# Attention with a gated feed-forward part on one Trainium2 core: two of three pattern operands of a score group added by an accumulating DMA

## The chip, the cores and the metric

The kernel runs on one core of a Trainium2 chip. A core has five engines that run their own instruction lists and wait for one another through semaphores: TensorE (PE; matmuls, its weight loads shown as PEld), VectorE (DVE), ScalarE (ACT), GpSimd (POOL) and SyncE (SP), which here only issues DMAs. Sixteen DMA engines move the data. The metric is the device time of one execution in microseconds, lower is better; the time given is the median of three runs.

## The reference

One block on 2048 tokens of width 512, all arrays bf16: a layer norm, then attention with 32 heads of width 16 and a gated feed-forward part of width 1792 beside it, both added to the input.

```python
def _A_ref(x, wqkv, wo):
    B, S, D = x.shape            # 1, 2048, 512
    H = 32; Dh = D // H          # 16
    qkv = (x @ wqkv).reshape(B, S, 3, H, Dh).transpose(2, 0, 3, 1, 4)
    q, k, v = qkv[0], qkv[1], qkv[2]
    scores = jnp.einsum("bhqd,bhkd->bhqk", q, k) * (Dh ** -0.5)
    p = _softmax(scores, axis=-1)
    o = jnp.einsum("bhqk,bhkd->bhqd", p, v)
    return o.transpose(0, 2, 1, 3).reshape(B, S, D) @ wo

def _B_ref(x, W_gate, W_up, W_down):
    gate = jnp.einsum("bsd,df->bsf", x, W_gate)
    up = jnp.einsum("bsd,df->bsf", x, W_up)
    h = gate * (gate > 0) * up
    return jnp.einsum("bsf,fd->bsd", h, W_down)

xn = _layernorm(x)
return x + _A_ref(xn, A_wqkv, A_wo) + _B_ref(xn, B_W_gate, B_W_up, B_W_down)
```

## The kernel before

**The work.** Attention is cut into 32 blocks: four stretches of 512 queries (`c4`), four sets of eight heads (`gg`), and two halves of each set (`ee`), so that a block has four heads. A block goes through 16 tiles of 128 keys (`kt`). For one key tile TensorE makes the scores of four heads, each 128 keys by 512 queries, in one PSUM bank of float32. The array is used in tiles of 64 rows by 32 columns: a score of one head is four matmuls in one half of the array, and the other half runs another one beside it. `matmul_loaded` (L136) issues one such matmul whose weights are already loaded; its tile size is fixed at 64x32.

**Two ways through the softmax.** A key tile takes one of two ways.

- *ScalarE.* Two exponentials (L1525) of 128x1024 each, `units` in the code, read two score banks each and write a slot of `ring`, a ring of `NRING` slots of 128x1024 bf16. Four matmuls in each half of the array then multiply the two slots with the values (`pv_stream`, L1405) and add into the block's PSUM bank. There are 708 such units.
- *VectorE.* The key tiles that `QUADS` and `dve_kt` choose, 158 in all (five in most blocks, six in six of them), go through `quad` (L1473), called a group here. Four instructions (L1481) turn four score banks into int16 numbers whose bits, read as bf16, are a power of two with a linear mantissa. Adding a constant to these bits gives the same curve shifted, and the sum of three shifted curves comes close to the exponential. So a group has three patterns of 128x2048: `raw`, `xa` (`raw` + 31) and `xb` (`raw` + 81). The two additions are made on GpSimd as 64-bit integer additions (L1495, `p3`), but on VectorE (L1498) for the first `FIRSTD` and last `LASTD` groups, two each. Each pattern is then multiplied with the values by itself, so the sum of the three curves is made in PSUM: three calls of `pv_stream`, 3 x 8 matmuls a group.

`raw` has `NRAW` = 4 slots and the other patterns `NPAT` = 5, all in the tensor `qd` (L650), 4 KB per partition and slot. A ring slot is 2 KB per partition.

**The other work.** Into the gaps go the projections of queries, keys and values, the feed-forward part (weights streamed in by SyncE's DMAs), the output projection, and at each block's end its normalisation, whose row sums come out of the value matmul.

**The order.** Nothing is ordered by hand. Every operation is entered with an engine, an estimated duration, what it reads and writes, and a priority. `Graph.run` (L212) then plays the program through: at each step the engine that can start earliest takes an operation, and with it buffer slots from the pools. A consumer of a GpSimd result may start at the producer's planned end (start, duration, latency `lat`) plus a slack; `PAT_SLACK`, 100 ns, for the value matmuls of a group. [...] `Graph.emit` (L443) writes the queues out as they were planned, with the semaphore waits that are needed. Each engine then runs its list strictly in that order, whatever the real durations are. SyncE's DMAs have a `stream` each, whose semaphore counts 16 for each transfer; `emit` recognises a DMA by its engine, `o.eng == "SP"`.

A group is entered `AHEAD` = 10 units before the unit at which its key tile stands, and its value matmuls have a priority one behind that unit.

**The opening.** TensorE starts with `heat` (L1018), ten matmuls of 128x128 weights and 512 columns of zeros into a bank that nobody reads; the plan gives it 4.5 us. While nothing else can run, `run` puts further blank matmuls of that kind into gaps (L1543). Then come the transposes of the normalised input (L858), the first projections and the first scores.

Of the kernel before, what the change touches and what calls it, by code (L numbers as in the profile page):

```python
# [5 lines left out]
BF16 = mybir.dt.bfloat16  # L6
# [6 lines left out]
ALU = mybir.AluOpType  # L13
# [13 lines left out]
EPS = 1e-5  # L27

BANK = (6, 7, 2, 3)
NRING = 16  # L30
PV_LAG = 1
BG_PRIO = 2
D1_PRIO = -500.0
# [10 lines left out]
NQ = 2  # L44
NWS = 2
NRAW = 4
NPAT = 5
LEAD = 15
QOFF = 0.3
EARLY = ()  # L50
# [3 lines left out]
FIRSTD = 2  # L54
TOGETHER = 0
LAST2 = 1
LASTD = 2
# [24 lines left out]
PV_EARLY = False  # L82
POOL_NS = 1060
LIB_NS = 7000
LANES = 0x0001000100010001
QUADS = [0, 3, 4, 5, 5, 6, 5, 5, 5, 5, 6, 5, 5, 5, 5, 6, 5, 5, 5, 6, 5, 5, 5, 5, 6, 5, 5, 5, 5, 6, 5, 5]

# [45 lines left out]
                 "load", "wsrc", "wkey", "wwaits", "pair")  # L133


def matmul_loaded(e, out, w, x, start, stop, at):  # L136

    return e.add_instruction(mybir.InstMatmult(  # L138
        name=e.bass.get_next_instruction_name(), engine=mybir.EngineType.PE, ins=[e.lower_ap(x), e.lower_ap(w)], outs=[e.lower_ap(out)],
        start_tensor_calc=start, stop_tensor_calc=stop, tile_size=(64, 32), tile_position=at, ldweights=False))  # L140


class Graph:
# [299 lines left out]
    def emit(self, nc, es):  # L443
        order = sorted(self.ops, key=lambda o: (o.start, o.idx))
        for o in self.ops:
            o.signal = o.eng == "SP"
            o.hb = None

        sems = {c: es.enter_context(nc.semaphore("s_" + c.lower())) for c in ("PE", "PEhi", "ACT", "DVE", "POOL")}
# [10 lines left out]
                held[o.half] = o.wkey  # L460

        def line(o):
            return o.stream if o.eng == "SP" else "PEhi" if o.eng == "PE" and o.half else o.eng
        for e in self.ENGS:
            n = {}
            for o in self.queue[e]:
# [10 lines left out]
        while left:  # L477
            moved = False
            for e in self.ENGS:
                q = self.queue[e]  # L480
                while pos[e] < len(q):
                    o = q[pos[e]]
                    if any(d.hb is None for d in o.deps):
                        break
                    k = known[e]
                    need = []
                    if e == "PE" and o.wsrc and o.load is not None:
                        o.wwaits = []
                        for d in sorted(o.wsrc, key=lambda d: -d.seq):
                            c = line(d)  # L490
                            v = d.val if d.eng == "SP" else d.cseq
                            if loads.get(c, -1) >= v:
                                continue
                            o.wwaits.append(d)
                            d.signal = True
                            for cc, vv in d.hb.items():
                                loads[cc] = max(loads.get(cc, -1), vv)
                                k[cc] = max(k.get(cc, -1), vv)
                    for d in sorted(o.deps, key=lambda d: -d.seq):
                        c = line(d)  # L500
                        v = d.val if d.eng == "SP" else d.cseq
                        if k.get(c, -1) >= v:
                            continue
                        need.append(d)
                        for cc, vv in d.hb.items():
                            if k.get(cc, -1) < vv:
                                k[cc] = vv
                    o.waits = need
                    for d in need:
                        d.signal = True  # L510
                    if e == "SP":
                        o.val = streams.get(o.stream, 0)
                        streams[o.stream] = o.val + 1
                        h = dict(k)
                        h[o.stream] = o.val
                    else:
                        h = dict(k)
                        h[line(o)] = o.cseq
                    o.hb = h
                    pos[e] += 1  # L520
                    left -= 1
                    moved = True
            assert moved, "cyclic order"
        dsem = {s: es.enter_context(nc.semaphore("d_%d" % i)) for i, s in enumerate(streams)}
        for e in self.ENGS:
            v = {}
            for o in self.queue[e]:
                if e == "SP":
                    o.sem = (dsem[o.stream], 16 * (o.val + 1))
                elif o.pair is not None:  # L530

                    o.sem = (pairs[o.pair % 2], 2 * (o.pair // 2 + 1))
                elif o.signal:
                    v[line(o)] = v.get(line(o), 0) + 1
                    o.sem = (sems[line(o)], v[line(o)])
# [11 lines left out]
        def play(e, eng):  # L547
            def wait(ds):
                best = {}
                for d in ds:  # L550
                    s, v = d.sem
                    if id(s) not in best or best[id(s)][1] < v:
                        best[id(s)] = (s, v)
                for s, v in best.values():
                    eng.wait_ge(s, v)
            loaded = set()
            for i, o in enumerate(self.queue[e]):
                if e == "SP" and i == end:
                    for s, v in done:
                        eng.wait_ge(s, v)  # L560
                if e == "PE" and o.load and o not in loaded:
                    wait(o.wwaits)
                    o.load(eng)
                if e == "PE" and o.load is not None and o.waits:

                    for q in self.queue[e][i + 1:i + 1 + self.AHEAD_LOADS]:
                        if q.load is None or q.wwaits or q in loaded:
                            break
                        if q.half != o.half:
                            if q.load:  # L570
                                q.load(eng)
                                loaded.add(q)
                            break
                wait(o.waits)
                ins = o.fn(eng)
                if e == "SP" or o.name == "st":
                    ins.then_inc(o.sem[0], 16)
                elif o.signal or o.pair is not None:
                    ins.then_inc(o.sem[0], 1)
            if e == "SP":  # L580
                for s, v in fin:
                    eng.wait_ge(s, v)
# [23 lines left out]
def bass_parallel_sum__mha_block__glu_gated_reglu__prompt_kernel(  # L606
# [13 lines left out]
    with ExitStack() as es:  # L620
        def sb(name, shape, dt):
# [20 lines left out]
        Wo_l = sb("Wo_l", [128, 2, D], BF16)  # L642
# [18 lines left out]
        ps = es.enter_context(nc.psum_tensor("ps", [128, 8, 512], FP32))  # L661

        G = Graph()
# [19 lines left out]
        zeros = Wo_l[:, 0, :]  # L683
# [5 lines left out]
             reads=[t_pid], writes=[t_pid], prio=-890)  # L689
        for v in (0, 2, 1, 3):  # L690
            G.op("DVE", 100, lambda e, v=v: e.tensor_scalar(hmask[:, v:v + 1], pid[:, 0:1], 16.0 * v, QSCALE, op0=ALU.is_equal, op1=ALU.mult),
                 reads=[t_pid], writes=[t_masks[v]], prio=-889 + v)
# [4 lines left out]
             reads=[t_id], writes=[t_id], prio=-898)  # L697
# [71 lines left out]
        for j in range(4):  # L769
            for ee in range(2):  # L770
                r0 = 32 * j + DH * ee
                dma(lambda e, r0=r0, ee=ee: e.dma_start(Wo_l[r0:r0 + DH, ee, :], A_wo[D - 128 + r0:D - 128 + r0 + DH, :]), 16,
                    reads=[t_woz], writes=[Tile()], prio=60, after=100)
# [4 lines left out]
        acc, junk = warm, up_sb[:, 0, 0:D // 2].bitcast(BF16)  # L778
# [213 lines left out]
        for n, bk in enumerate(blocks):  # L992
            q = QUADS[n]
            dve_kt[bk] = [int((a + QOFF) * NT / q * (LAST_QUADS if n == len(blocks) - 1 else 1.0)) for a in range(q)] if n else EARLY
            if n:
                at = sorted({min(max(t + QUAD_SHIFT.get((n, a), 0), 0), NT - 1) for a, t in enumerate(dve_kt[bk])})
                if len(at) == len(dve_kt[bk]):
                    dve_kt[bk] = at
        kinds = {}
# [5 lines left out]
        at_unit, n = [], 0  # L1005
# [11 lines left out]

        def heat(e):  # L1018
            ins = None
            for _ in range(10):  # L1020
                ins = e.matmul(ps[:, BANK[0], :], Wo_l[:, 0, 0:128], zeros, start=True, stop=True)
            return ins
        G.op("PE", 4500, heat, reads=[t_zero], writes=[t_pvz], prio=-900)
        ln_block(0, -800)
        pb = Tile("pro", P_b, [3])
# [31 lines left out]
        for v in (0, 2, 1, 3):  # L1057
# [3 lines left out]
            for n, (tile, bank, c, x) in enumerate(((pb, 3, slice(0, 384), slice(0, 384)), (bq, 1, slice(128, 256), slice(384, 512)))):  # L1061
# [4 lines left out]
                     reads=[tile, t_masks[v]], writes=[] if n else [t1], joins=[q0], prio=MASK_LATE + v if late else -787 + 0.2 * v + 0.1 * n,  # L1066
# [153 lines left out]
        at, rest = 40.0, sum(j[1] for j in seq[:-4])  # L1220
        for w, n, fn, lead in seq:
            at = max(at, w)
# [250 lines left out]
        def quad(key, u, prev):  # L1473
# [4 lines left out]
            for j in SC_ORDER:  # L1478
# [4 lines left out]
                    reads=[tx], joins=[tq], prio=D1_PRIO, name="d1")  # L1483
# [5 lines left out]
            ta, xa = made("qa")  # L1489
            tb, xb = made("qb")  # L1490
            nq[0] += 1
            for n, (t, x) in enumerate(((ta, xa), (tb, xb))):
                share, off = ((POOL1_SHARE, P1_OFF), (POOL_SHARE, 0.0))[n] if FIRSTD < nq[0] <= len(kinds) - LASTD else (0.0, 0.0)
                if int(nq[0] * share + off) > int((nq[0] - 1) * share + off):
                    G.op("POOL", POOL_NS, lambda e, x=x, n=n: e.int64_add(x().bitcast(I64), raw().bitcast(I64), SHIFTS[n + 1] * LANES),  # L1495
                        reads=[ti, tq, t_lib], writes=[t], prio=u, name="p3", port=True)
                    continue
                G.op("DVE", 600, lambda e, n=n, x=x: e.tensor_scalar(x(), raw(), float(SHIFTS[n + 1]), None, op0=ALU.add),  # L1498
                     reads=[ti, tq], writes=[t], prio=u, name="d%d" % (n + 2), port=True)
            first = len(G.ops)  # L1500
            for t, x, more in ((ti, raw, [tq]), (ta, xa, []), (tb, xb, [])):
                pv_stream(key[:3], key[3], [(lambda rows, j=j, x=x: x()[rows, 512 * j:512 * j + 512].bitcast(BF16)) for j in range(4)],
                          [t] + more, u, u + PV_LAG, "DVE")
            if TOGETHER:
# [2 lines left out]
                        o.order |= set((ta if TOGETHER == 1 else tb).w)  # L1507
            return prev

        nq = [0]  # L1510
        quads = sorted((at_unit[place[k]], place[k], k) for k in kinds)
        prev_sc, prev_d, made_q = None, None, 0
        for u, unit in enumerate(units):
            while li < len(plan) and plan[li][0] <= u:
# [4 lines left out]
            key, p = unit[:4], unit[4]  # L1519
            k0 = u % 2  # L1520
            ts = Tile("s%d" % u, P_sc, [k0])
            for sub in range(2):
# [3 lines left out]
                              reads=[ts], writes=[tr], prio=u - 100, order=[exp_ops[u - 1]] if u else [], name="ex%d" % u)  # L1526
# [54 lines left out]
```

## Time and profile before

| what | value |
|---|---|
| median of three runs | 684.08 us (683.42 to 684.76) |
| the profiled execution, whole | 682.77 us |
| its span, first to last instruction | 680.6 us |
| granted TensorE clock, mean | 1.00 |
| DMA: moved; mean rate | 28.77 MB; 42 GB/s |
| first exponential starts; last ends | 10.3 us; 669.5 us |

The profile is one execution. Its span leaves out what lies before the first and after the last instruction. A busy time counts the time in which at least one instruction of the engine runs, so instructions that overlap in the pipeline are not counted twice: the mean duration of one exponential, 1117 ns, is longer than its share of the busy time, 651.9 / 708 = 0.921 us. In a group's row the idle time stands behind the bar, with the instruction that ended most of it. PE, PEld, DVE, ACT, POOL and SP are the engines as named above.

### The profile page before, as it was taken

The page shows a single profiled execution, that of the slowest core. Times are in us where ns is not written, and L with a number is a line of the kernel's source. Part 1 is how long each engine was busy: PE and PEld are TensorE (multiplying, and loading weights), DVE is VectorE, ACT ScalarE, POOL GpSimd, SP SyncE. Part 2 cuts the span into 40 slices and gives each one's busy share as a digit, 9 for nine tenths or more (in the row PEclk, how much of TensorE's full clock was granted, in tenths as well). Part 3 has the DMA queues.
Part 4 walks back from the last instruction along what each step waited for, and adds up shares of the span by engine and source line. Part 5 has one row for each costly group of instructions (what it writes and reads, how often), then busy time and mean ns, then how long its engine had stood idle before and what let it go on. Part 6 is the DMA issues. An engine that isn't in the chain of part 4 may idle for free.

```text
span 680.6 us, 46065 instructions
## 1 busy us (share of the span) xinstructions
PE 671.9 (99%) x22322; PEld 397.0 (58%) x20890; DVE 587.0 (86%) x993; ACT 659.8 (97%) x725; POOL 330.8 (49%) x341
## 2 busy tenths in 40 slices
PE   8999999999999999999999999999999999999997
PEld 3565665557565556566655656655555665655574
DVE  8957997999999878888999886889999887998876
ACT  7999999999999999999999999999999999999984
POOL 3302443564556555544556654445556654546540
PEclk9999999999999999999999999999999999999999
DMA  6520011133200121010101111110100121120001
GB/s 202 88 51 21 19 38 42 46 90 80 69 21 21 37 57 44 21 37 16 41 10 23 42 46 50 26 40 22 35 5 21 36 78 33 43 60 13 21 13 35
DMA packets 51478, 28.77 MB, mean 42 GB/s; under 512 B 18840, under 2 KB 50328, under 8 KB 51288
## 3 DMA queue, kind: packets, MB, share of 16 engines
q1 hardware_dynamic: 51144, 25.70, 14.8%
q8 instruction: 169, 2.77, 1.7%
q14 instruction: 21, 0.17, 0.1%
q10 hardware_dynamic: 144, 0.13, 0.1%
HBM read 18.22 MB, written 2.10 MB: 30 GB/s over the span
## 4 chain that ended last, share of the span: by engine, by line
PE 85%; ACT 10%; DVE 4%; issue 0%; DMA 0%; POOL 0%; DVEq 0%
PE ps L138 85%; ACT ring L1525 10%; DVE stats L810 1%; DMA x_sb<-in_A_x_dram 0%; DVE qd L1481 0%; DVE xn_sb L833 0%; DVE qd L1498 0%; DVE mv L812 0%; DVE xn_sb L1298 0%; POOL rstd L794 0%; DVE v_aug L978 0%; DVE kT L971 0%; DVE xnT L878 0%; DVE qT L1065 0%; DVE up_sb L1277 0%
## 5 line engine op out<-in xcount | busy, mean ns | idle before, releaser
L1525 ACT ACTIVATE ring<-ps 128x1024 bf16<-128x1024 f32 x708 | 651.9, 1117 | 7.3 <-PE ps L138 6.5
L1495 POOL INT64_ADD qd<-qd x308 | 317.3, 1040 | 308.9 <-DVE qd L1481 173.5
L138 PE MATMUL ps<-qT,kT 64*32 64x512 bf16 x8192 | 464.5, 375 | 1.2 <-DVE kT L971 0.4
L1481 DVE TENSOR_SCALAR qd<-ps 128x512 int16<-128x512 f32 x632 | 412.8, 684 | 59.6 <-PE ps L138 53.0
L138 PE MATMUL ps<-qd,v_aug 64*32 64x512 bf16 x3792 | 302.2, 375 | 0.2
L138 PE MATMUL ps<-ring,v_aug 64*32 64x512 bf16 x2832 | 242.4, 375 | 0.1
L1461 PEld LDWEIGHTS <-kT 64*32 64x32 bf16 x8132 | 175.3, 92 | 110.0 <-issue 24.4
L1433 PEld LDWEIGHTS <-v_aug 64*32 64x32 bf16 x5252 | 128.6, 92 | 63.9 <-issue 10.1
L138 PE MATMUL ps<-xnT,wgs 64*32 64x512 bf16 x1792 | 137.0, 375 | 0.0
L138 PE MATMUL ps<-xnT,wus 64*32 64x512 bf16 x1792 | 135.3, 375 | 0.0
L138 PE MATMUL ps<-Wd,hT 64*32 64x512 bf16 x768 | 58.6, 375 | 0.3 <-issue 0.2
L913 PEld LDWEIGHTS <-hT 64*32 64x32 bf16 x1792 | 43.9, 92 | 24.1 <-issue 3.7
L913 PEld LDWEIGHTS <-wgs 64*32 64x32 bf16 x1792 | 43.7, 92 | 22.8 <-issue 3.5
L913 PEld LDWEIGHTS <-wus 64*32 64x32 bf16 x1792 | 43.8, 92 | 22.5 <-issue 3.3
L1130 DVE COPY up_sb<-ps 128x512 f32<-128x512 f32 x56 | 38.3, 685 | 7.3 <-PE ps L138 7.3
L138 PE MATMUL ps<-Wv,hT 64*32 64x512 bf16 x512 | 40.3, 375 | 0.4 <-issue 0.4
L1134 DVE SCALAR_TENSOR_TENSOR hT<-ps,up_sb 128x512 bf16<-128x512 f32 x56 | 38.3, 683 | 2.7 <-PE ps L138 2.5
L138 PE MATMUL ps<-Wk,hT 64*32 64x512 bf16 x512 | 39.6, 375 | 0.0
L138 PE MATMUL ps<-Wo_p,x_sb 64*32 64x512 bf16 x480 | 37.7, 376 | 0.1
L138 PE MATMUL ps<-xnT,Wq 64*32 64x512 bf16 x480 | 37.1, 375 | 0.0
L138 PE MATMUL ps<-xnT,Wk 64*32 64x512 bf16 x480 | 35.9, 375 | 0.3 <-DVE xnT L878 0.3
L138 PE MATMUL ps<-Wv,xnT 64*32 64x512 bf16 x512 | 30.4, 375 | 0.3
(83 smaller groups left out, 222.3 us busy)
## 6 DMA issues: line engine op xcount, KB each, us to landing
wus<-in_B_W_up_dram SPq DMA_DIRECT2D x38, 128.0 KB, 2.4
wgs<-in_B_W_gate_dram SPq DMA_DIRECT2D x38, 128.0 KB, 2.5
xr_sb<-in_A_x_dram SPq DMA_DIRECT2D x16, 128.0 KB, 2.7
qT<-qf SPq DMA_DIRECT2D x120, 16.0 KB, 2.3
o_sb<-o_sb SPq DMA_DIRECT2D x60, 32.0 KB, 2.6
out_dram<-xn_sb SPq DMA_DIRECT2D x15, 128.0 KB, 1.9
x_sb<-in_A_x_dram SPq DMA_DIRECT2D x8, 128.0 KB, 2.7
Wd<-in_B_W_down_dram SPq DMA_DIRECT2D x6, 128.0 KB, 2.7
```

Of the source, the lines that this page charges most:

```text
L138: return e.add_instruction(mybir.InstMatmult(name=e.bass.get_next_instruction_name(), engine=mybir.EngineType.PE, ins=[e.lower_ap(x), e.lo ...
L810: G.op("DVE", 580, lambda e, m=m: e.bn_stats(stats[:, m, :], xs(m)), reads=[t_xm[m]], writes=[t_st], prio=pr, order=last_xn if m == 4 and ...
L913: e.ldweights(w()[rows, 32 * j:32 * j + 32], tile_position=(rows.start, 32 * j))
L1130: G.op("DVE", 603, lambda e: e.tensor_copy(up_sb[:, tup.slot, :], bank_of(tu)), reads=[tu], writes=[tup], prio=-590)
L1134: G.op("DVE", 603, lambda e: e.scalar_tensor_tensor(out=hT[:, th.slot, :], in0=bank_of(tg), scalar=0.0, in1=up_sb[:, tup.slot, :], op0=ALU ...
L1433: e.ldweights(vs(j), tile_position=(64 * half, 32 * j))
L1461: e.ldweights(ks(m), tile_position=(64 * half, 32 * m))
L1481: G.op("DVE", 601, lambda e, j=j, tx=tx: e.tensor_scalar(qd[:, tq.slot, 512 * j:512 * j + 512], ps[:, BANK[tx.slot], :], IBIAS[3], 0.0, op ...
L1495: G.op("POOL", POOL_NS, lambda e, x=x, n=n: e.int64_add(x().bitcast(I64), raw().bitcast(I64), SHIFTS[n + 1] * LANES), reads=[ti, tq, t_lib ...
L1525: exp_ops[u] = G.op("ACT", 904, lambda e, tr=tr, k0=k0: e.activation(ring[:, tr.slot, :, :], ps[:, 4 * k0:4 * k0 + 2, :], ACTF.Exp, scale= ...
```

## The change

Three things change.

1. For all groups but the first two and the last two, `kinds[k]` is 2. In such a group GpSimd, after making `xa` and `xb`, issues a DMA that adds `xa` into `xb` (as bf16, 128 rows of 2048), and only `raw` and `xb` go through the value matmuls. The DMA is entered with 1000 ns on GpSimd and a latency of 5500 ns, with four semaphores taken in turn, and each waits for the one four before. `emit` now recognises a DMA by its stream, as GpSimd has some too. The pattern slots become six, one more.
2. `ring` has 14 slots instead of 16, which frees the room of the sixth pattern slot.
3. `heat` issues five of the blank matmuls instead of ten, and behind them loads 32x32 weights into the sixteen tiles of the array and runs four rounds of sixteen matmuls of 512 columns on them. Its planned duration stays 4.5 us.

The integers that GpSimd adds, the thresholds and the choice of key tiles stay as they are. The sum of the second and third curve is now rounded to bf16 once before the matmul.

```diff
-NRING = 16
+NRING = 14
-NPAT = 5
+NPAT = 6
+ACC_NS, ACC_LAT, NACC = 1000, 5500.0, 4
...
-def matmul_loaded(e, out, w, x, start, stop, at):
+def matmul_loaded(e, out, w, x, start, stop, at, size=(64, 32)):
...
-        start_tensor_calc=start, stop_tensor_calc=stop, tile_size=(64, 32), tile_position=at, ldweights=False))
+        start_tensor_calc=start, stop_tensor_calc=stop, tile_size=size, tile_position=at, ldweights=False))
...
-            o.signal = o.eng == "SP"
+            o.signal = o.stream is not None
...
         def heat(e):
             ins = None
-            for _ in range(10):
+            for _ in range(5):
                 ins = e.matmul(ps[:, BANK[0], :], Wo_l[:, 0, 0:128], zeros, start=True, stop=True)
+            at = [(32 * r, 32 * c) for r in range(4) for c in range(4)]
+            for r, c in at:
+                e.ldweights(Wo_l[r:r + 32, 0, 0:32], tile_position=(r, c))
+            for _ in range(4):
+                for r, c in at:
+                    ins = matmul_loaded(e, ps[c:c + 32, BANK[r // 32], :], Wo_l[r:r + 32, 0, 0:32], zeros[r:r + 32, :], True, True, (r, c), (32, 32))
             return ins
...
             first = len(G.ops)
+            if kinds[key] == 2:
+                G.op("POOL", ACC_NS, lambda e: e.dma_start(xb().bitcast(BF16), xa().bitcast(BF16), accum_op=ALU.add),
+                     reads=[ta], writes=[tb], prio=u, name="acc", port=True, stream=("acc", len(accs) % NACC), lat=ACC_LAT)
+                if len(accs) >= NACC:
+                    G.ops[-1].deps[accs[-NACC]] = True
+                accs.append(G.ops[-1])
             for t, x, more in ((ti, raw, [tq]), (ta, xa, []), (tb, xb, [])):
+                if t is ta and kinds[key] == 2:
+                    continue
                 pv_stream(key[:3], key[3], [(lambda rows, j=j, x=x: x()[rows, 512 * j:512 * j + 512].bitcast(BF16)) for j in range(4)],
...
-        nq = [0]
+        nq, accs = [0], []
         quads = sorted((at_unit[place[k]], place[k], k) for k in kinds)
+        for n, (_, _, k) in enumerate(quads):
+            kinds[k] = 2 if FIRSTD <= n < len(kinds) - LASTD else 3
```

The remaining lines of the diff replace `o.eng == "SP"` by `o.stream is not None` in the same way in `emit`.

More of the change, by code (lines that the diff above doesn't have):

```diff
@@ L462, in line @@
         def line(o):
-            return o.stream if o.eng == "SP" else "PEhi" if o.eng == "PE" and o.half else o.eng
+            return o.stream if o.stream is not None else "PEhi" if o.eng == "PE" and o.half else o.eng
         for e in self.ENGS:
@@ L490, in emit @@
                             c = line(d)
-                            v = d.val if d.eng == "SP" else d.cseq
+                            v = d.val if d.stream is not None else d.cseq
                             if loads.get(c, -1) >= v:
@@ L500, in emit @@
                         c = line(d)
-                        v = d.val if d.eng == "SP" else d.cseq
+                        v = d.val if d.stream is not None else d.cseq
                         if k.get(c, -1) >= v:
@@ L510, in emit @@
                         d.signal = True
-                    if e == "SP":
+                    if o.stream is not None:
                         o.val = streams.get(o.stream, 0)
@@ L527, in emit @@
             for o in self.queue[e]:
-                if e == "SP":
+                if o.stream is not None:
                     o.sem = (dsem[o.stream], 16 * (o.val + 1))
@@ L575, in play @@
                 ins = o.fn(eng)
-                if e == "SP" or o.name == "st":
+                if o.stream is not None or o.name == "st":
                     ins.then_inc(o.sem[0], 16)
```

## The prediction

> **What bounds the kernel now.** I read the page's first part, then its groups, then the waits of each engine, then single stretches of the timeline. A measurement of this kernel can tell about 0.2% (1.4 us) from no change. The first part has the busy time of each engine.
>
> ```profile
> PE 671.9 (99%) x22322; PEld 397.0 (58%) x20890; DVE 587.0 (86%) x993; ACT 659.8 (97%) x725; POOL 330.8 (49%) x341
> ```
>
> Two engines look full. The groups (busy time, mean of one, then idle time before them and who ended it) tell them apart.
>
> ```profile
> L1525 ACT ACTIVATE ring<-ps 128x1024 bf16<-128x1024 f32 x708 | 651.9, 1117 | 7.3 <-PE ps L138 6.5
> L1495 POOL INT64_ADD qd<-qd x308 | 317.3, 1040 | 308.9 <-DVE qd L1481 173.5
> L1481 DVE TENSOR_SCALAR qd<-ps 128x512 int16<-128x512 f32 x632 | 412.8, 684 | 59.6 <-PE ps L138 53.0
> L138 PE MATMUL ps<-qd,v_aug 64*32 64x512 bf16 x3792 | 302.2, 375 | 0.2
> ```
>
> ScalarE's 708 exponentials fill 651.9 us, 0.921 us each, and it waits 7.3 us for them in the whole run. Its first exponential starts at 10.3 us and its last ends at 669.5; the other 11.1 us are the end of the program. 10.3 + 651.9 + 7.3 + 11.1 = 680.6, the span: ScalarE's row alone accounts for all of it. The waits of ScalarE from 45 to 640 us (engine, line, what it waited for; total, times, longest) are nearly nothing:
>
> ```profile
> ACT ring L1525 <- PE ps L138: 1.4, 6, 0.4
> ```
>
> Of the remaining waits on TensorE 2.2 us lie before 45 us and 2.8 us in one place, at 653.7 us. TensorE's 99% is another thing. In the timeline one half of the array takes its next four matmuls after 0.21 to 0.22 us:
>
> ```profile
> 649.75 0.38 PE L138 MATMUL ps<-qd,v_aug 64*32 64x512 bf16 x4
> 649.80 0.38 PE L138 MATMUL ps<-Wv,hT 64*32 64x512 bf16 x4
> 649.97 0.38 PE L138 MATMUL ps<-qd,v_aug 64*32 64x512 bf16 x4
> 650.02 0.38 PE L138 MATMUL ps<-Wv,hT 64*32 64x512 bf16 x4
> 650.18 0.38 PE L138 MATMUL ps<-Wd,hT 64*32 64x512 bf16 x4
> ```
>
> The step of 0.215 us for eight matmuls (two halves) is its pace when fed. From 56 to 662 us it ran 20,480 matmuls in 606 us, where 20,480 / 8 x 0.215 = 550 us would do: it is 91% loaded, with 56 us of slack lost in pieces too short to see. [...] If the 99% were the bound, the sum below would be 33 us instead of 4; that is a rival, judged by ScalarE's row.
>
> **The change, part by part.**
>
> *Removed.* 158 groups have three patterns of eight matmuls each (3,792). 154 of them lose one: 1,232 matmuls, 154 x 0.215 = 33 us of TensorE, 6% of its fed work; 91% load becomes 85%. None of that is on ScalarE, whose 708 exponentials stay (the list of groups per block is not touched). What it can win is ScalarE's waiting on TensorE. Middle of the run: 1.4 us, all taken. The place at 653.7 us: 2.8 us, where TensorE runs groups together with the final output rows; half of it taken, 1.4 (bounds 0 and 2.8). Small lateness inside "busy": the commonest distance between two ends of exponentials is 917 ns, 708 x 0.917 = 649.2 against 651.9, so 2.7 us; half, 1.3 (bounds 0 and 2.7). Opening: 2.2 us, nothing taken, as GpSimd's first addition for a group starts at 56 us and VectorE still does the first two groups. Sum -4.1, at most -6.9.
>
> *Added on GpSimd.* 154 issues of an accumulating DMA. No row shows one. Nearest below: SyncE's issue of a plain DMA, 0.43 us. Above: GpSimd's own INT64_ADD, 1.04 us, since both are work of its cores for 128 rows. I take 1.0, the nearer engine. Two additions and one issue are 2 x 1.04 + 1.0 = 3.1 us a group; groups come every 4.2 us in the mean (3.07 us in the six blocks that have six groups: ten other key tiles, 20 exponentials of 0.921 us, 18.4 us for six). GpSimd goes from 52% to 78% of the stretch from 56 to 662 us (317.3 + 154 = 471 of 606). It has 309 us of idle time before those additions now. Queued behind each issue are only the next group's additions, and what waits for these is the second pattern's matmuls.
>
> *Added on the DMA engines.* Each accumulate moves 512 KB, 128 rows of 4 KB, eight rows for each of 16 engines. The trace's 2 KB packets take 82 ns at best and 112 in the median, so eight 4 KB rows are 1.3 to 1.8 us, and, as the destination is read too, up to twice that: 1.3 to 3.6 us. 154 of them: 200 to 550 us of 680 on engines that are 17% busy now. Small transfers land after 2.3 us:
>
> ```profile
> qT<-qf SPq DMA_DIRECT2D x120, 16.0 KB, 2.3
> o_sb<-o_sb SPq DMA_DIRECT2D x60, 32.0 KB, 2.6
> Wv<-in_A_wqkv_dram SPq DMA_DIRECT2D x1, 512.0 KB, 5.3
> ```
>
> So an accumulate lands 2.3 + 1.3 = 3.6 to 2.3 + 3.6 = 5.9 us after its issue; the one plain 512 KB load in the list took 5.3, in the crowded opening. I take 4.7, the middle. The kernel's own plan puts the matmuls of the sum 1.0 + 5.5 + 0.1 us after the issue starts, so at 4.7 nothing is late: price 0. At 5.9 TensorE, which runs its list strictly in order, stands 0.4 us, and with it the scores queued behind; ScalarE has one finished pair of score banks to live on, 0.92 us.
>
> *Moved.* The sum's matmuls come later than the third pattern's did. Now they end 5.5 us (median) after the second addition, and 1.3 us at the least; the plan needs 6.6 after. So the median group moves by about 1 to 2 us, which is two exponentials of lag in a block of 20 or 22. The two patterns are held 8.7 us (two additions, issue and landing) and about 9.6 us (one addition, 6.6, wait and matmul): 18.3 us in six slots is one group in 3.05 us, against 4.2 needed, and 3.07 in the six-group blocks. Price 0, with no reserve there.
>
> *Ring of 14 pairs.* Counting exponentials begun against pairs of key tiles multiplied, the ring held more than 14 at 11 of 354 releases (about 36 to 41, 160 to 173, 637 to 639 and 657 us), and nine in the median. Some of these cost a short wait: +0.5 (0 to +2, at 0.2 us for each).
>
> *Opening.* Ten blank matmuls run from 1.18 us, 0.427 us apart; five remain, 2.1 us. Four rounds of sixteen 32x32 matmuls are 4 x 0.427 = 1.7 us if sixteen run side by side, as eight 64x32 ones do in one 0.375 us row, and double that, 3.4, if only eight can. With some 0.2 us of weight loads they end at 5.2 or 6.9 us; the transposes need TensorE at 5.84 us, when it has just become fast (128 columns in 56 ns, where the blank ones took 427 for 512). So 0 to +1.1 us; I take 0. Should it stay slow in the opening, VectorE's chain (10.3 us to the first exponential) still covers most of it.
>
> *Sum.* -1.4 - 1.4 - 1.3 + 0.5 + 0 + 0 = -3.6 us. On the profiled span 680.6 that is 677.0. The profiled execution took 682.8 us in all, 2.2 more than its span, and the median of the three timed runs is 684.1, 1.3 more again; 684.1 - 3.6 = **680.5 us**. Its own range runs from 684.1 - 6.9 = 677.2 to about 683.
>
> **The rivals.**
>
> *Nothing comes through (0.15).* ScalarE's row sets the time, and the four microseconds are given back to the ring and the new order: 684 within 1.4 us. For it: only 1.4 us of waiting in 595. Against: 33 us of room for TensorE can hardly leave every wait as it was.
>
> *Late accumulates (0.22), the other side.* Place: the matmuls of the sum in TensorE's list. An accumulate that meets another one or a 128 KB weight load waits for it, 1.3 us or more: 5.9 + 1.3 = 7.2, 1.7 us later than the plan. ScalarE lives through 0.9 of it and loses 0.8. Groups are some 13 us long (3.4 to make, 2.2 of additions, 6.6, and the matmul) and come every 4.2, so one stall serves three: 51 stalls. If half of them meet something, 26 x 0.8 = 21 us: 705; if all, 725. It decides from a landing of 6.4 us (5.5 + 0.9). For it: the upper bound of the landing is already past 5.5, and weights load all through the run. Against: the middle is 4.7.
>
> *Patterns held too long (0.12).* If both are held 1.5 us longer than reckoned, six slots give a group in 3.5 us; a six-group block is then 2.8 us late, six blocks 17 us, of which the lead of ten exponentials hides perhaps two thirds: +6, 690.
>
> *TensorE is the bound (0.03).* All 33 us come off: 651. ScalarE's 651.9 + 21.4 us of opening and end speak against it.
>
> *Code is loaded each time (0.04).* Before GpSimd's first 64-bit addition the trace has 5.7 us, and before its last stock instruction 7.1 us, that nothing explains:
>
> ```profile
> POOL ints L1538 <- issue: 7.1, 1, 7.1
> POOL ints L886 <- issue: 5.7, 1, 5.7
> ```
>
> If the DMA's descriptors were made by code outside the loaded library, each group would pay both: 154 x (12.8 + 2.1 + 0.4) = 2,360 us, about 2,440 with what stands around it. Against: MEMSET and CAST ran within 3 us of the first 64-bit addition without it. [...]
>
> **How the numbers follow.** The forecast has 0.44. Faster: 0.44 + 0.03 = 0.47. Same: 0.15. Slower: 0.22 + 0.12 + 0.04 = 0.38. The range 676.5 to 705 holds the forecast, the first and third rivals and half of the second, 0.82; left out are 651, 2,440 and the worse half of the late accumulates.
>
> **What would show it.** Right: 2,560 matmuls from qd instead of 3,792; ScalarE's 708 exponentials still about 0.92 us each, its wait on TensorE from 45 to 640 us under 1 us; GpSimd's accumulates landing within 5.5 us; the first exponential still at 10.3 us. Wrong: TensorE or its weight loads waiting for the accumulate by name, ScalarE idle in pieces over 0.5 us through the middle, GpSimd with unexplained gaps of 6 us, or the first transposes later than 5.9 us.

## The result and the profile after

The changed kernel takes 811.21 us in the median (806.85 to 818.54, three runs) against 684.08 before: a ratio of 1.187, 95% interval 1.182 to 1.191. It is 127 us slower, far outside the predicted range. The profiled execution took 818.54 us, its span is 816.7. For e2 and e4 below, whose two runs lie 2% apart, the time is that of the faster run (788.29 and 735.04 us; the others took 803.03 and 750.62), and e4's profile is of the slower. First the busy times of the change, then the groups that answer to those of before (busy time and mean, then idle time and who ended it).

```profile
PE 699.7 (86%) x21149; PEld 386.5 (47%) x20941; DVE 590.1 (72%) x993; ACT 673.6 (82%) x725; POOL 466.5 (57%) x495
...
L1542 ACT ACTIVATE ring<-ps 128x1024 bf16<-128x1024 f32 x708 | 665.7, 1055 | 120.5 <-PE ps L139 119.0
...
L1502 POOL INT64_ADD qd<-qd x308 | 331.8, 1111 | 251.3 <-DVE qd L1488 197.1
...
L139 PE MATMUL ps<-qd,v_aug 64*32 64x512 bf16 x2560 | 242.0, 387 | 18.2 <-issue 12.6
...
L1509 POOL DMA_DIRECT2D qd<-qd x154 | 136.3, 885 | 55.4 <-POOL qd L1502 35.6
```

The change did what it says: 2,560 matmuls read `qd` instead of 3,792, and 154 accumulates were issued. But ScalarE, which waited 7.3 us before, now waits 120.5, nearly all for TensorE. So TensorE, with 6% less to do, is late. The waits (total, times, longest) say for whom TensorE waited:

```profile
...
ACT ring L1542 <- PE ps L139: 119.0, 112, 5.5
PEld L1468 <- issue: 86.7, 178, 5.6
PE ps L139 <- issue: 72.8, 59, 2.5
PEld L1440 <- issue: 60.4, 95, 5.5
...
DVE rb L1403 <- DMA rb<-rrec: 14.6, 5, 6.0
...
PE ps L139 <- DMA qd<-qd: 4.8, 1, 4.8
```

For an accumulate, by name, 4.8 us once. For "issue", that is for nothing that a semaphore shows, far more. One such stop, on TensorE's rows and then ScalarE's:

```profile
117.92 0.38 PE L139 MATMUL ps<-xnT,wgs 64*32 64x512 bf16 x4
117.93 0.38 PE L139 MATMUL ps<-qT,kT 64*32 64x512 bf16 x3
120.84 0.38 PE L139 MATMUL ps<-qT,kT 64*32 64x512 bf16 x5 [2.54 <-issue]
```

```profile
114.97 3.77 ACT L1542 ACTIVATE ring<-ps 128x1024 bf16<-128x1024 f32 x4 [0.29 <-PE ps L139]
121.29 1.02 ACT L1542 ACTIVATE ring<-ps 128x1024 bf16<-128x1024 f32 x1 [2.55 <-PE ps L139]
```

Where it falls is what tells: three of the four matmuls of one score have run, and the fourth comes 2.9 us later. The four stand behind one wait, so no semaphore lies between them. What is between them is the end of a block of instructions. The long stops of TensorE come after its 5,056th, 6,336th, 6,592nd, 7,360th instruction and so on, all 192 more than a multiple of 256. Over 1 us passes between the starts of two of its instructions 56 times, 49 of them at such a place; before the change it is twice, and never there. The row of the queue that carries instructions, in the profile of before (packets, MB, share of 16 DMA engines), gives the size: 169 packets of 16 KB, one for every 256 of TensorE's 43,300 instructions.

```profile
q8 instruction: 169, 2.77, 1.7%
```

And the queues after, with the accumulates in the first row:

```profile
q0 software_dynamic: 22176, 80.75, 53.3%
q1 hardware_dynamic: 51144, 25.70, 12.3%
q8 instruction: 165, 2.70, 1.4%
```

I worked out from single start times, in both traces, how a block reaches TensorE. Stops at the blocks' ends are distances of over 0.3 us from the last instruction of a block to the first of the next:

| | before | after |
|---|---|---|
| a block lasts (median) | 3.85 us | 4.59 us |
| its fetch starts after the block before it began: median; 75%; 95% | 0.97; 1.15; 1.56 us | 1.59; 2.89; 3.80 us |
| the fetch takes (median) | 1.12 us | 0.98 us |
| from the fetch's end to the block's first instruction: least; median | 1.23; 1.76 us | 1.24; 1.47 us |
| stops at the blocks' ends, in all | 4.7 us | 114.0 us |

The fetch itself is no longer than it was, and the 1.2 us after it are the same; it **starts late**. Before, TensorE had a reserve of 1.76 - 1.23 = 0.5 us per block. After, 81 blocks stop TensorE for over 0.3 us, and 80 of these begin 1.2 to 1.6 us after the end of their own fetch; this fetch started 2.7 us (median) after the block before it began, that of the other blocks 1.1 us. Accumulate packets run for 535 of the 816.7 us, so that 111 of the 165 fetches start while they run is no more than chance would give. But these 111 start, in the median, 3.3 us after such a run of packets began and 0.46 us before it ends, as they would if they stood behind it. One accumulate is nine packets on each of 16 engines (154 x 16 x 9 = 22,176, the first row), eight of 4 KB with 338 ns each, 2.7 us, and one of 4 bytes.

That a fetch stands behind a whole run of accumulate packets is read from these start times; in what order a DMA engine takes its queues, no trace and no run of this case shows.

### The profile page after: what moved, and what is told of

The parts are those of the page before. It is cut to its first block, busy times and chain, and to the rows that moved or that the text cites. A ratio compares the mean times of both kernels' runs of the same rounds, so it can differ in the third digit from the quotient of the medians.

```text
span 816.7 us, 45127 instructions
## 1 busy us (share of the span) xinstructions
PE 699.7 (86%) x21149; PEld 386.5 (47%) x20941; DVE 590.1 (72%) x993; ACT 673.6 (82%) x725; POOL 466.5 (57%) x495
## 3 DMA queue, kind: packets, MB, share of 16 engines
q0 software_dynamic: 22176, 80.75, 53.3%
## 4 chain that ended last, share of the span: by engine, by line
PE 58%; ACT 15%; issue 11%; DVE 8%; SPq 5%; DMA 3%; POOL 0%; DVEq 0%; POOLq 0%
PE ps L139 58%; ACT ring L1542 14%; DVE qd L1488 4%; SPq L962 2%; SPq L1382 2%; DMA rb<-rrec 2%; DVE stats L811 1%; DMA qd<-qd 1%; DVE up_sb L1137 0%; DVE hT L1141 0%; DMA x_sb<-in_A_x_dram 0%; DVE rb L1403 0%; DVE o_sb L1350 0%; SPq L1391 0%; POOL qd L1502 0%
## 5 line engine op out<-in xcount | busy, mean ns | idle before, releaser
L1542 ACT ACTIVATE ring<-ps 128x1024 bf16<-128x1024 f32 x708 | 665.7, 1055 | 120.5 <-PE ps L139 119.0
L139 PE MATMUL ps<-qT,kT 64*32 64x512 bf16 x8192 | 496.1, 386 | 59.7 <-issue 32.0
L1502 POOL INT64_ADD qd<-qd x308 | 331.8, 1111 | 251.3 <-DVE qd L1488 197.1
L139 PE MATMUL ps<-ring,v_aug 64*32 64x512 bf16 x2832 | 262.9, 387 | 11.1 <-issue 9.8
L1468 PEld LDWEIGHTS <-kT 64*32 64x32 bf16 x8112 | 184.5, 94 | 169.2 <-issue 86.7
L139 PE MATMUL ps<-qd,v_aug 64*32 64x512 bf16 x2560 | 242.0, 387 | 18.2 <-issue 12.6
L1440 PEld LDWEIGHTS <-v_aug 64*32 64x32 bf16 x5312 | 136.4, 94 | 113.0 <-issue 60.4
L1509 POOL DMA_DIRECT2D qd<-qd x154 | 136.3, 885 | 55.4 <-POOL qd L1502 35.6
L139 PE MATMUL ps<-xnT,wgs 64*32 64x512 bf16 x1792 | 144.5, 387 | 7.4 <-issue 7.3
L139 PE MATMUL ps<-Wv,hT 64*32 64x512 bf16 x512 | 45.2, 387 | 2.6 <-issue 2.5
L139 PE MATMUL ps<-Wo_p,x_sb 64*32 64x512 bf16 x480 | 41.1, 386 | 0.0
```

The source lines that it names most:

```text
L139: return e.add_instruction(mybir.InstMatmult(name=e.bass.get_next_instruction_name(), engine=mybir.EngineType.PE, ins=[e.lower_ap(x), e.lo ...
L1440: e.ldweights(vs(j), tile_position=(64 * half, 32 * j))
L1468: e.ldweights(ks(m), tile_position=(64 * half, 32 * m))
L1509: G.op("POOL", ACC_NS, lambda e: e.dma_start(xb().bitcast(BF16), xa().bitcast(BF16), accum_op=ALU.add), reads=[ta], writes=[tb], prio=u, n ...
L1542: exp_ops[u] = G.op("ACT", 904, lambda e, tr=tr, k0=k0: e.activation(ring[:, tr.slot, :, :], ps[:, 4 * k0:4 * k0 + 2, :], ACTF.Exp, scale= ...
```

## The experiments

Every time of before in the same chip session lay between 683.0 and 684.7 us (median), so 684 is used. "Stops" are TensorE's at the blocks' ends in the run's profile. F (the fetch of instructions is held up), L (the sum lands late), N (SyncE's transfers are held up) and P (ring, opening or plan) are the theories named in the first expectation.

| run | time, us | stops, us | accumulates' share of DMA engines |
|---|---|---|---|
| before | 684.1 | 4.7 | - |
| the change | 811.2 | 114.0 | 53.3% |
| e1: no accumulate | 685.8 | 10.0 | - |
| e2c: ring of 12, control | 692.6 | under 5 | - |
| e2: traffic alone | 788.3 | 98.1 | 55.3% |
| e3: plain copy | 714.9 | 37.6 | 29.0% |
| e9: rows 0-63; rows 64-127 | 788.0; 787.2 | 83.2; 82.4 | 49.2%; 49.4% |
| e7: planned later | 870.8 | 83.7 | 50.2% |
| e4: every second group | 735.0 | 75.9 | 29.2% |
| e10: every second, two DMAs | 732.3 | 41.1 | 33.3% |
| e5: every second, four DMAs | 772.6 | 26.8 | 36.9% |
| e6: all groups, two DMAs | 828.0 | 57.8 | 58.0% |

**e1, the change without its accumulates.**

```diff
-            kinds[k] = 2 if FIRSTD <= n < len(kinds) - LASTD else 3
+            kinds[k] = 3
```

> The changed kernel with all 158 groups back at three patterns and no accumulate; ring of 14, six pattern slots and the new opening stay. Theories: (F) the accumulates' packets hold up the 16 KB instruction blocks that TensorE fetches, one for every 256 of its instructions; (L) the matmuls of the sum wait for accumulates that land late; (N) the accumulates delay SyncE's transfers for the normalisation and the queries; (P) the ring of 14, the opening or the new order of the plan cost the time. F, L and N: 684 +- 4 us. P: over 780.

685.84 us, ratio 1.0037 (1.0019 to 1.0055). The ring of 14, the opening and the new order cost some 2.5 us together; P falls.

**e8, the opening alone** on the kernel of before (the new `heat`, nothing else).

> The kernel of before with the new opening alone (five blank matmuls and 64 small ones instead of ten). All theories: the same as before within 1.5 us; first exponential at 10.3 to 10.5 us.

685.43 us, ratio 1.0008 (0.9989 to 1.0027): no difference. In the changed kernel the 64 small matmuls run in 1.9 us, sixteen side by side (in the trace they start in four groups of sixteen, at 3.45, 3.83, 4.26 and 4.68 us, each group within 0.03 us), and the first transposes start at 5.77 us, so nothing waited for them.

```profile
1.18 2.32 PE L1022 MATMUL ps<-Wo_l 128*128 128x512 bf16 x5 [1.18 <-DVE warm L686]
3.45 1.89 PE L139 MATMUL ps<-Wo_l 32*32 32x512 bf16 x64
...
5.77 0.40 PE L859 MATMUL ps<-ident,xn_sb 128*128 128x128 bf16 x4
```

**e2 and e2c, the traffic alone, and its control.** All groups keep three patterns; an accumulate of the same size goes into two spare buffers in turn.

```diff
-            kinds[k] = 2 if FIRSTD <= n < len(kinds) - LASTD else 3
+            kinds[k] = 3
+            noise.add(k) if FIRSTD <= n < len(kinds) - LASTD else None
...
-            if kinds[key] == 2:
-                G.op("POOL", ACC_NS, lambda e: e.dma_start(xb().bitcast(BF16), xa().bitcast(BF16), accum_op=ALU.add),
-                     reads=[ta], writes=[tb], prio=u, name="acc", ...
+            if key in noise:
+                G.op("POOL", ACC_NS, lambda e, i=NRAW + NPAT + len(accs) % 2: e.dma_start(qd[:, i, :].bitcast(BF16), xa().bitcast(BF16), accum_op=ALU.add),
+                     reads=[ta, t_scr], writes=[], prio=u, name="acc", ...
```

> Traffic alone: three patterns in all groups as before, five pattern slots, and 154 accumulating DMAs of the same size from the second pattern into two spare buffers that nobody reads; only the buffer's next user waits. The ring has 12 slots to make room. TensorE's work is that of before. F: as slow as the changed kernel or slower, 790 to 850 us, gaps at every 256th TensorE instruction adding up to 100 us or more. N: slower by some 30 us through the waits on row sums. L: the same as its control without the DMAs, within 10 us.

> Control of the run with traffic alone: the same buffers and ring of 12, no accumulating DMA. F, L, N: 684 to 692 us. P with the ring as cause: clearly over that.

788.29 us against the control's 692.62 (690.73 and 694.52): 96 us for DMAs whose results nobody reads. Between the two profiled spans, 786.3 and 688.8, lie 97.5 us, and the stops went from under 5 to 98.1. TensorE's waits in the run with traffic, then in the control:

```profile
...
ACT ring L1547 <- PE ps L139: 98.3, 104, 3.9
...
PEld L1468 <- issue: 65.7, 130, 3.1
PE ps L139 <- issue: 62.0, 54, 2.7
...
DVE rb L1403 <- DMA rb<-rrec: 8.6, 3, 4.1
```

```profile
...
PEld L1468 <- issue: 30.4, 114, 0.8
ACT ring L1547 <- PE ps L139: 15.3, 15, 4.2
```

This is the run that decides. No matmul waits for the sum, so L cannot make it; N's wait for the row sums (last line of the first fence) is 8.6 us. TensorE has the work of its control, so the sums can be set side by side: 94 us more of stops, 97.5 us more of span. All 75 blocks that begin over 0.3 us late begin 1.2 to 1.6 us after the end of their own fetch. The time is 1.7 us under F's range. The control is 0.6 us over its own, ratio 1.013 (1.009 to 1.017): a ring of 12 costs about 9 us.

**e7, the sum planned later.** `ACC_LAT` 9000 instead of 5500.

> The changed kernel with the accumulate's planned latency raised from 5.5 to 9 us, so that the matmuls of the sum stand later in TensorE's list. L: most of the loss gone, under 720 us. F: no better, 790 to 840 us, with the same gaps at every 256th instruction.

870.82 us, ratio 1.274 (1.267 to 1.280), worse than the change by 60 us: L's forecast fails. F's range was too low as well; the stops are there, 83.7 us, but more than they was lost. The patterns are held longer, and GpSimd waits for matmuls to free the slots:

```profile
POOL qd L1502 <- PE ps L139: 196.7, 93, 6.6
```

In the changed kernel that row has 36.4 us. So the third rival of the prediction, patterns held too long, may be what costs here, at a latency of 9 us. It is not shown: the kernel of before has 132.6 us of the same wait and loses nothing by it, and the granted clock is 0.940 here against 0.961. As a late plan brings a loss of its own, this run alone would not refute L; e2 does.

**e3, a plain copy in place of the accumulate.** The third pattern is overwritten by the second.

```diff
-e.dma_start(xb().bitcast(BF16), xa().bitcast(BF16), accum_op=ALU.add)
+e.dma_start(xb().bitcast(BF16), xa().bitcast(BF16))
```

> The changed kernel with a plain copy of the second pattern over the third in place of the accumulate (the third pattern is left out of the sum): same issue, same waits, same 512 KB. By the rows of before a 4 KB packet of a plain copy should take about 165 to 220 ns instead of the accumulate's 338, so an engine's eight packets 1.3 to 1.8 us instead of 2.7. F: the fetch waits for a shorter burst, loss less than half, 700 to 750 us. L: near 684, as it lands early. If only the number of DMAs mattered: 811.

714.92 us, ratio 1.045 (1.026 to 1.063), as F said. The bytes are the same, the time they take on the engines is about half: 160 ns for 4 KB instead of 338.

```profile
q0 software_dynamic: 22176, 80.75, 29.0%
...
qd<-qd POOLq DMA_DIRECT2D x154, 512.0 KB, 3.5
```

**e9, half of the rows.** Two kernels, one with rows 0 to 63 in the accumulate, one with rows 64 to 127.

```diff
-e.dma_start(xb().bitcast(BF16), xa().bitcast(BF16), accum_op=ALU.add)
+e.dma_start(xb()[0:64, :].bitcast(BF16), xa()[0:64, :].bitcast(BF16), accum_op=ALU.add)
```

> The accumulate covers rows 0 to 63 alone (256 KB; the second pattern is left out of the sum for rows 64 to 127). Half the bytes, and if a row's place decides which DMA engine moves it, half of the engines with full bursts of 2.7 us and half with none. F with TensorE's fetch always on the same engines: this run and the one on rows 64 to 127 differ strongly, one near 690 us without gaps at every 256th instruction, the other near 800. F with the fetch going round all engines: both about 735 to 760 us. F with the load of all engines as cause: both alike and below that, near the plain copy's 715.

> The accumulate covers rows 64 to 127 alone (the second pattern is left out of the sum for rows 0 to 63). As for rows 0 to 63: with the fetch on fixed engines one of the two near 690 and the other near 800 us; with the fetch going round, both 735 to 760.

787.97 and 787.16 us: alike, and slower than any of the three forecasts for alike. The reason is in the queue's row (that of rows 0 to 63):

```profile
q0 software_dynamic: 12320, 40.38, 49.2%
...
qd<-qd POOLq DMA_DIRECT2D x154, 256.0 KB, 4.7
```

Half the bytes hold the engines for nearly as long: 64 rows of 4 KB are four for each of 16 engines, and each takes 651 ns instead of 338, so a burst is 2.6 us again (a run of its packets lasts 2.8 us in the median). So a row's place did not choose the engine (12,320 packets are 154 x 16 x 5, four rows and one of 4 bytes), and whether the fetch sits on certain engines stays open. But with e3 the run tells bytes from engine time: all the bytes in half the time cost 31 us (37.6 of stops), half the bytes in all the time 104 (83 of stops).

**e4, e10, e5 and e6, fewer or smaller accumulates.** e4 sums only every second group. e10 and e5 cut e4's accumulates into two and four DMAs of 1024 and 512 columns, e6 cuts all 154 into two.

```diff
-            kinds[k] = 2 if FIRSTD <= n < len(kinds) - LASTD else 3
+            kinds[k] = 2 if FIRSTD <= n < len(kinds) - LASTD and n % 2 == 0 else 3
...
+                for h in range(4):
+                    G.op("POOL", ACC_NS, lambda e, c=slice(512 * h, 512 * h + 512): e.dma_start(xb()[:, c].bitcast(BF16), xa()[:, c].bitcast(BF16), accum_op=ALU.add),
...
```

> Only every second of the 154 groups is summed by an accumulate, the others keep three patterns. F: a fetch meets a burst half as often, loss about half or less, 720 to 750 us. N: about half too. L: half or less.

> Every second group, each accumulate cut into two DMAs of 1024 columns: the bytes of the run with every second group (743 us), bursts half as long, and GpSimd with room for its extra issues (two issues and four additions in two groups' time of 8.5 us). F with the burst's length as what counts: gaps at every 256th instruction down from 76 to about 35 us, time 700 to 722 us. If bytes alone count: 735 to 750 us. If the extra issues count more than the bursts: 750 us or more.

> As the run with every second group, but each accumulate is cut into four DMAs of 512 columns (same bytes, packets of 1 KB, four times the issues on GpSimd). If the DMA engine finishes the packets of one DMA before it turns to the instruction fetch (F with a turn per DMA), the fetch waits a quarter as long: 684 to 705 us, and the gaps at every 256th instruction nearly gone. If bytes alone count (N, or F with the engine's load as cause): as the run with one DMA, or worse by GpSimd's extra issues.

> All 154 groups, each accumulate cut into two DMAs of 1024 columns. F with a turn per DMA: the fetch's wait is halved to about 1.4 us against a reserve of some 0.5 us, so more than half of the loss goes, 700 to 745 us. If bytes alone count: 800 us or more.

e4 took 735.04 us. e10 took 732.34 us, ratio 1.070 (1.065 to 1.076), e5 772.59 (1.129; 1.118 to 1.140), e6 828.03 (1.210; 1.202 to 1.218). e4 is within its range; the times of the other three missed what F with a turn per DMA said of them, e10 by 10 us. By time alone the rival "bytes alone count" did better: e5 and e6 came out as it said, and e10 is 2.7 us under its range. But e9 with e3 speaks against bytes, and the stops did fall as F said: cut in two, from 114.0 to 57.8 us over all groups, though the accumulates hold the engines for 58.0% of the time instead of 53.3%. With four pieces, at every second group, they are 26.8. So the stops go with the time that the packets of one DMA take on an engine (2.7 us in the change; 8 x 185 ns = 1.5 in e6; 1.3 in e3, which has 37.6 us of stops) more than with the sum over all DMAs.

But e6 and e5 are slower, not faster, than the uncut change and the uncut e4. In e5 GpSimd has become full with the additions and the issues:

```profile
L1502 POOL INT64_ADD qd<-qd x308 | 414.6, 1945 | 92.6 <-DVE qd L1488 55.4 <-PE ps L139 23.0 <-DVE x_sb L1406 13.3
...
L1511 POOL DMA_DIRECT2D qd<-qd x308 | 286.6, 1523 | 30.9 <-DVE x_sb L1406 22.2 <-POOL qd L1502 8.6
```

GpSimd is busy with these two for 701 of 768 us, and an addition takes 1945 ns beside the issues instead of 1040. That GpSimd ate the gain in e5 and e6 (694 us busy there) is a guess from these sums and not shown: no run took GpSimd's load away, and no row of TensorE's waits in e5 and e6 names a pattern of GpSimd. A lower granted clock, 0.954 in e6 and 0.982 in e5, is another candidate. Between e4 and e10 the times leave open whether cutting helps at all.

No version here beats the kernel of before.

## Why the prediction was wrong

- *What bounds the kernel.* That ScalarE's row sets the time of the kernel before is what its page shows (7.3 us of waits). That 33 us less on TensorE could give only a few was never tested, as no run has the relief without traffic. The 56 us of TensorE's slack "lost in pieces too short to see" hold 4.7 us of stops at the blocks' ends; where the rest goes no run shows. What counted was hidden beside it: a fetch that came only 0.5 us before its block was due.
- *Removed.* The count was right. With no accumulates (e1) nothing is gained either, as the matmuls are back. The relief by itself was never seen on the clock: the traffic covers it.
- *Added on GpSimd.* 1.0 us taken, 0.885 measured. Right, though the reason given, work for 128 rows, is not borne out: with 64 rows an issue still takes 0.833 us (e9).
- *Added on the DMA engines.* 1.3 to 3.6 us per accumulate and engine said, 2.7 measured; 200 to 550 us of the engines' time, 0.533 x 816.7 = 435 measured; landing 3.6 to 5.9 us, 5.6 measured. All inside the bounds, though the landing is 0.9 over the 4.7 that was taken and over the 5.5 named as a sign of being right:

```profile
qd<-qd POOLq DMA_DIRECT2D x154, 512.0 KB, 5.6
wus<-in_B_W_up_dram SPq DMA_DIRECT2D x38, 128.0 KB, 3.7
...
qT<-qf SPq DMA_DIRECT2D x120, 16.0 KB, 3.9
```

- **The step that failed** is the next sentence, "nothing is late: price 0". It asked only whether the sum itself would land in time, and it nearly always did: TensorE waited once for an accumulate. The load on the engines was priced by its own landing and by what two accumulates or a weight load do to each other. TensorE's instruction blocks, which the page counts among the traffic of the same 16 engines, were in none of the terms, though the page of before had their row (169 packets, 2.77 MB). That term measures 114 - 5 = 109 us, where 136 us lie between the profiled spans; in e2, with TensorE's work unchanged, it is 94 of 97.5.
- *The other side's rival.* "Late accumulates" had the right sign and 0.22, but another place (the matmuls of the sum) and price (705 to 725). e2 loses 96 us with no matmul that waits for a sum, and in the change that wait is 4.8 us, so its mechanism is not what costs.
- *What else is in the 136 us.* SyncE's transfers do suffer, 3.9 us instead of 2.3 for the queries in the fence above. Twice this stops TensorE for over 5 us. At 240 us seven issues for the queries run on until 240.3, the reciprocals go out behind them, VectorE waits for them and TensorE for VectorE (SyncE's rows, VectorE's, TensorE's):

```profile
232.56 7.72 SPq L962 DMA_DIRECT2D qT<-qf  x7
240.32 1.27 SPq L1391 DMA_DIRECT2D rb<-rrec  x2
```

```profile
245.44 0.01 DVE L1403 LOAD_MASK_SELECT rb<-rb  x1 [5.26 <-DMA rb<-rrec]
```

```profile
246.78 0.58 PE L139 MATMUL ps<-qT,kT 64*32 64x512 bf16 x4 [5.16 <-DVE qd L1488]
```

  A second such stop, 5.3 us, begins at 621 us. These 10.5 us and the 109 above are sizes and do not add up to a full account of the 136, because two more things pull in opposite ways. TensorE has 33 us less to do. And its granted clock is 0.961 in this profile instead of 1.00, lowest in the stretches with the two long stops (0.87 from 240 to 280 us, 0.91 from 600 to 640); the trace has it at half in 15 stretches of 66 us in all. As an estimate from the mean, that costs TensorE at most 0.039 x 816.7 = 32 us. No run separates the two.
- *Ring and opening.* +0.5 and 0 said; e1 has 2.5 us for both and the new order, e8 puts the opening at nothing.
- *Code loaded each time.* The 154 issues have 2.6 us of unexplained idle time before them in all, so that price was not paid. What fills the 5.7 and 7.1 us of before (6.0 and 7.4 after the change) no run shows.
- *Readings that were off, without bearing on the miss.* "The one plain 512 KB load" was one of two: another, into `hT`, took 6.6 us in the same list, more than the upper bound of 5.9. SyncE's issues take 0.59 us in the median; 0.43 was that of two loads in the opening. A group came every 606 / 154 = 3.9 us and not every 4.2, so the six slots had less reserve than was reckoned.

## What to carry to other kernels

Read the row of the instruction queue before adding DMA traffic: here TensorE's instructions came in a stream of 16 KB blocks, 169 before the change and 165 after, and when its reserve (0.5 us in 3.85) was used up, it waited, 114 us in all, without a semaphore that shows it. Price a DMA by the time for which it holds the engines at one stretch (here 2.7 us), not by bytes or landing alone, and ask of everything else on those engines what it costs to come that much later. When an engine that lost work gets slower, look at what its stops have in common: here multiples of 256 instructions between them (49 of the 56 distances of over 1 us) pointed to a fetch and not to a dependency.

## What was not expected of the hardware

- An accumulating DMA within SBUF took 338 ns for a 4 KB row on an engine (the change), a plain copy 160 (e3).
- With 64 rows instead of 128 each row took 651 ns (e9), so that half of the bytes held the engines as long (49.2% against 53.3%).
- Issuing the accumulate cost GpSimd 885 ns (the change), the plain copy 551 (e3); with 308 issues in e5 the 64-bit additions beside them went from 1040 to 1945 ns.
